# Another order ahead of the first exp in a transformer block kernel: K maxima, transposed tiles, and one copy of K and one of V between ScalarE and VectorE

## The chip, the cores and the metric

The kernel runs on one core of a Trainium2 chip. Its engines work from queues of their own, each strictly in the order of its program, and wait for each other by semaphores: PE (TensorE, matmuls into the eight banks of PSUM), DVE (VectorE), ACT (ScalarE), POOL (GpSimd) and SP (SyncE, which issues the transfers). The metric is the device time of one execution in microseconds, as the median of several runs.

## The reference, cut to what matters

One transformer block in bfloat16 with 2048 tokens of width 640, 32 heads of width 20, and a gated feed-forward part of width 1728.

```python
def _A_ref(x, wqkv, wo):
    qkv = (x @ wqkv).reshape(B, S, 3, H, Dh).transpose(2, 0, 3, 1, 4)
    q, k, v = qkv[0], qkv[1], qkv[2]
    scores = jnp.einsum("bhqd,bhkd->bhqk", q, k) * (Dh ** -0.5)
    p = _softmax(scores, axis=-1)
    o = jnp.einsum("bhqk,bhkd->bhqd", p, v)
    return o.transpose(0, 2, 1, 3).reshape(B, S, D) @ wo

h = x + _A_ref(_layernorm(x), A_wqkv, A_wo)
h2 = h + (gelu(_layernorm(h) @ w_gate) * (_layernorm(h) @ w_up)) @ w_down
```

## The kernel before

**A list scheduler writes the program.** The kernel's Python code describes some 6,900 operations with an engine, an estimated duration, a priority (a smaller number goes first), what they read and write, and the PSUM banks that they take and free. `Sched.schedule` (L100 to L272) plays them through on estimated times and so fixes the order on each engine; `emit` (L274) writes that order with its semaphore waits. On the chip the order is fixed, the times are not: an instruction that waits holds everything behind it on its engine.

**Units and slots.** The scores of 128 keys by 512 queries of one head, or an equal area with fewer queries, are a tile of one PSUM bank. A unit (L1045) takes two or three tiles: PE computes the scores (L1069, four heads at a time in rows of 32 partitions), ACT does one exp over all of them into `pts` or the second ring, which lies in `rege`, and PE multiplies the result with V (PV, recorded at L440). Some tiles go to DVE instead, which forms the exponential out of integer operations (L982 and further rows of L440). Units are grouped into 32 slots by the chunk of queries and the group of four heads: slots 0 to 7 are the first 512 queries, one group of heads each; 8 to 27 are five chunks of 256; 28 to 31 are two of 128. In the profile slot 0 begins at 35.19 us, slot 4 at 134.1, slot 14 at 381.01, and the last exp ends at 842.05. The projections for later heads, the output projection and the feed-forward part of each finished chunk of queries run as background work between the units; the last chunk's stand alone behind the last exp.

**How the scheduler sets the order.** A score matmul has priority 0. When an exp is placed, `due` (L254) is the time from which PE has to stay free for the next scores, `QK_LEAD` ahead of it; background work that would run past `due` is put off. PE has three modes (full, four rows, four columns) with a cost for changing; an operation in another mode is put off until it has waited longer than `PE_AGE` (L177). `SD_AGE` and `SD_ROW` do the same for the scores of DVE's tiles. Each of these is a tuple with an entry per slot.

**Ahead of the first exp.** The normalised input (16 tiles of 128 tokens, `xnp`) is transposed by PE (L665) and copied out of PSUM into `xnT` by ACT (L671) or, for the tiles in `XN_DVE`, by DVE (L674). The first K tile (`proj_k(0)`: the rows of the first heads, all 2048 tokens) is computed in four chunks of 512 tokens, the last cut into 384 and 128 (`KCUT`); each chunk needs the four transposed tiles of its tokens. ACT copies it to SBUF (L785), and DVE takes the maximum of its absolute values (L782): for chunks 0 and 1 from SBUF, for chunks 2 and 3 (`KPS`) from PSUM ahead of ACT's copy, which waits for it. The maximum over the five parts (`kd`, L835) scales a selection matrix (`sel0`, L837); a matmul with it (L881) and a DVE sum (L885, written `('qo', 0, 0)`) give the bound that is subtracted inside the first scores. Only then can the first score matmul run. An exp needs another function table than the copies and square roots before it, so a table load stands in ACT's queue directly in front of the first exp.

The second K tile (`proj_k(1)`, into `osb`) and the second Q tile are computed while this goes on; their copies on DVE wait for the sum of L885 (`HELD`), and chunk 0 of the second K tile was given to ACT (`K1_ACT`, L790). V is projected three token tiles at a time for the first heads (L897); its copies are on DVE (L907), the ones from tile `V_HOLD` on waiting for `HELD` too. SP issues the transfers that spread Q and K over the partitions in the order of its queue: four for Q, one to `q_rows`, sixteen for the first K tile, then the rows of the later tiles.

Of the kernel before, what the change touches and what calls it, by code (L numbers as in the profile page):

```python
# [18 lines left out]
DRAIN = {"pe": 0.165, "act": 0.118, "dve": 0.085, "pool": 0.05, "sp": 0.0}  # L19
WARM_WIN, WARM_MIN = 3.4, 0.5  # L20
PAD_WIN, PAD_MIN = 3.4, 0.42
QK_LEAD = (0.68, 0.72,) + (0.65,) * 4 + (0.72,) * 7 + (0.6,) * 4 + (0.72,) * 6 + (0.68,) * 9
ACT_GAP = .012
PE_AGE = (2.5, 3.0, 5.0, 5.0, 2.5,) + (1.0,) * 4 + (2.0,) + (5.0,) * 3 + (3.0,) * 4 + (5.0, 5.0, 2.0, 2.0,) + (5.0,) * 4 + (1.5, 1.5, 3.5, 3.0,) + (1.5,) * 3
SD_AGE = (0.6, 0.6, 0.3,) + (0.6,) * 6 + (0.8,) + (0.6,) * 5 + (1.0, 0.3, 0.6, 0.8, 0.6, 1.0, 0.5, 1.0, 1.0, 0.5,) + (0.6,) * 7
SD_ROW = (0,) * 5 + (1.0,) + (0.6,) * 3 + (1.5, 0.6, 0.6, 1.5,) + (0.6,) * 16 + (1.0, 0.6, 0,)
STOP = None


# [22 lines left out]
class Sched:  # L52
# [3 lines left out]
    def __init__(self, nc):  # L56
        self.nc = nc
        self.ops = []
        self.lw = {}
        self.rd = {}  # L60
        self.warm = None
        self.pad = None
        self.final = set()
        self.ev = 9
# [35 lines left out]
    def schedule(self):  # L100
# [5 lines left out]
        free_at = [0.0] * 8  # L106
        owner = [None] * 8
# [4 lines left out]
        mode = {e: None for e in ENGINES}  # L112
# [6 lines left out]
        t = 0.0  # L119
# [5 lines left out]
        cur = 0  # L125
        at = lambda v: v[cur] if isinstance(v, tuple) else v
        total = len(ops)
        scores = sum(o.eng == "pe" and o.mode == "row" for o in ops)
        while done < total:
            assert events, "no operation can start"  # L130
# [5 lines left out]
            for e in ENGINES:  # L136
# [8 lines left out]
                while ready[e]:  # L145
                    p, i = heapq.heappop(ready[e])
                    o = ops[i]
                    got = []
                    if e == "pe" and due is not None and o.prio[0] > 0 and t < due < t + o.dur + (MODE_SWITCH[e] if mode[e] not in (None, o.mode) else 0):
                        skipped.append((p, i))  # L150
                        if due not in events:
                            heapq.heappush(events, due)
                        if len(skipped) >= 60:
                            break
                        continue
                    for bk in o.acq:
                        for b in bk.allowed if scores else bk.allowed + bk.after:
                            if owner[b] is None and free_at[b] <= t + 1e-9 and b not in got and b not in kept:
                                got.append(b)
                                break  # L160
                        else:
                            got = None
                            break
                    if got and o.mode == "row" and 0 < p[0] < 1 and scores > 1 and t - o.ready < (
                            at(SD_AGE) if mode[e] != "row" else at(SD_ROW) if row_end[o.rows[0]] > max([row_start + 0.01] + [freed[b] for b in got]) + 0.02 else 0):
                        skipped.append((p, i))
                        continue
                    if got is None:

                        if p[0] == 0:  # L170
                            kept.update(bk.allowed[0] for bk in o.acq)
                        skipped.append((p, i))
                        continue
                    skipped.append((p, i))
                    if chosen is None:
                        chosen, banks = o, got
                        if e != "pe" or p[0] < 1 or p[0] == P_NOW or o.mode == mode[e] or t - o.ready > at(PE_AGE):  # L177
                            break
                    elif o.mode == mode[e]:
                        chosen, banks = o, got  # L180
                        break
                    if len(skipped) >= 60:
                        break
# [34 lines left out]
                scores -= o.eng == "pe" and o.mode == "row"  # L218
                if o.tag and o.tag[0] == "S":
                    cur = self.slot_of[o.tag[1]]  # L220
                if e == "pe" and self.pad is not None and o.tag and o.tag[0] in ("O", "Oq"):
# [146 lines left out]
WN, WB, WW, WC = 76, (5, 4), 256, 32  # L368
KCUT = (384,)
KPS = (2, 3)  # L370
P_VA = 9
VN = 4
D_RING = (9,) * 4 + (6, 6,) + (9,) * 6 + (6,) * 16 + (12,) + (6,) * 3
D_FIRST = 0
# [10 lines left out]
P_V1 = 3.0  # L385
P_V0 = 2.5
P_ON = 2.1
V_ACT = ()
XN_DVE = (8, 10, 13, 15)
VP = (0, 2, 5, 8)  # L390
V1 = ((0, 0, 0, 0, 0, 0, 0, 0, 1, 1, 1, 1, 1, 1, 1, 1), (2, 2, 2, 2, 3, 3, 3, 3, 3, 3, 3, 3, 4, 4, 4, 4))
X_LAT = 3.0
# [4 lines left out]
P_KP = 1.6  # L397
K1_AFTER = 3
Q1_HOLD = 1
V_HOLD = 4  # L400
XD = ()
P_NOW = 1.05
P_K0 = 1.0
VB = (6, 7, 5)
K1_ACT = (0,)
FULL = (5,)
GROUPS = ((0, 4), (4, 7), (11, 5))
AG = (11, 5)
# [10 lines left out]
def bass_sequential_preLN__mha_block__glu_gated_geglu__prompt_kernel(  # L419
# [12 lines left out]
    with ExitStack() as es:  # L432
# [340 lines left out]
        def proj_part(col, t, c, dst, dkey, banks, prio, evac, after, start, lo, hi, k):  # L773
# [6 lines left out]
                                   [("xnT", tt) for tt in range(4 * c + lo // 128, 4 * c + hi // 128)] + ["wqk"], prio, after=start))  # L780
            if dkey[0] == "ku" and t == 0:
                red = lambda src, r: op("dve", lambda eng: eng.tensor_reduce(km[:, c + k:c + k + 1], src(), AX.X, ALU.max, apply_absolute_value=True),  # L782
                                        0.62 if n == 512 else 0.1 + n * 0.00102, P_K0, reads=[r], writes=[("km", c + k)])
                m = [red(lambda: bank(bk, n), key)] if c in KPS else []
                e = op("act", lambda eng: eng.activation(dst, bank(bk, n), ACT.Copy), c_act(n), prio, reads=[key],  # L785
                       writes=[dkey], rel=[bk], after=m)
                if c not in KPS:
                    w_readers.append(red(lambda: dst, dkey))
            elif evac == "act":
                e = op("act", lambda eng: eng.activation(dst, bank(bk, n), ACT.Copy), c_act(n), prio, reads=[key],  # L790
                       writes=[dkey], rel=[bk])
# [253 lines left out]
        def unit(u):  # L1045
# [11 lines left out]
            xd = dtile[u]  # L1057
            six = ring[u]
            al = tl + ([xd] if six else [])
            bks = [Bank(s0 + i) for i in range(len(al))]  # L1060
            fns = []
            reads = []
# [22 lines left out]
            qk = op("pe", fns, 0.215, P_QK, mode="row", util=0.0533 * len(al), rows=tuple(x[3] for x in al), reads=reads, writes=[("S", u), "qkseq"] + ([("SD", xd)] if six else []), acq=bks)  # L1085
            for x in al:
                last_qk[CHUNKS[slots[x[0]][0]][0] // 512].append(qk)
            if six:
# [422 lines left out]
```

## Time and profile before

| | us |
|---|---|
| median of 3 runs (lowest, highest) | 869.43 (868.62, 869.72) |
| the profiled execution, its time | 868.33 |
| its span, first to last instruction | 866.6 |
| ACT busy | 838.3 |
| DVE busy | 748.9 |
| PE busy | 830.7 |

The granted clock of TensorE is 0.998 of full speed on average. A row of the timeline reads: start in us, length in us, engine, line, operation, the tiles written and read with their shapes, the count of equal instructions merged into it, and in brackets how long the engine stood idle before it and what ended that. Instructions of one engine overlap at their ends, so the bars of a merged row add up to more than the time from one start to the next. A row of the busy times by stage reads: the stretch, its length, then busy time and count on PE, on PE's weight loads, on DVE, ACT and POOL, the clock, the share of the DMA engines and GB/s. SPq are the transfers as SP issues them.

### The profile page before, as it was taken

The numbers are of one execution on the slowest core, as the hardware profiler recorded it, in microseconds if no ns is written. First come the engines' busy times: TensorE is split into PE (matmuls) and PEld (weight loads), VectorE is DVE, ScalarE is ACT, GpSimd is POOL, SyncE is SP. The second block draws the span as 40 slices with busy tenths as digits, with TensorE's granted clock in tenths as the row PEclk, the third lists the DMA queues.
The fourth block names the chain that finished last, engine by engine and source line by source line (L and its number), as shares of the span: only waits on it lengthen the run. The fifth ranks groups of instructions, "written<-read, shape, count | busy, mean of one in ns | idle before, by whom it ended". The sixth has DMA issues, their size and how long they took to land.

```text
span 866.6 us, 35475 instructions
## 1 busy us (share of the span) xinstructions
PE 830.7 (96%) x16164; PEld 421.4 (49%) x16199; DVE 748.9 (86%) x1372; ACT 838.3 (97%) x806; POOL 92.2 (11%) x268
## 2 busy tenths in 40 slices
PE   7999999999999899999999999999999999999998
PEld 5533322322344344445455555555554556666667
DVE  8759899999899789697899989999999897998344
ACT  7899999999999999999999999999999999999992
POOL 5001111110001210101102010011102110010000
PEclk9999999999999999999999999999999999999999
DMA  7211122113201752001111201010111201020000
GB/s 273 82 46 59 32 76 61 40 61 93 64 10 46 166 156 83 16 16 30 58 33 28 36 8 61 3 36 16 37 32 19 56 17 28 19 48 11 2 18 17
DMA packets 50173, 43.19 MB, mean 50 GB/s; under 512 B 21316, under 2 KB 44640, under 8 KB 50024
## 3 DMA queue, kind: packets, MB, share of 16 engines
q1 hardware_dynamic: 50024, 40.93, 16.9%
q8 instruction: 127, 2.08, 1.0%
q14 instruction: 22, 0.18, 0.1%
HBM read 27.95 MB, written 10.26 MB: 44 GB/s over the span
## 4 chain that ended last, share of the span: by engine, by line
ACT 57%; PE 35%; DVE 7%; issue 1%
ACT pts L440 38%; ACT rege L440 17%; PE ps L1069 10%; PE ps L743 9%; PE ps L440 8%; PE ps L748 2%; DVE qt_all L440 2%; PE ps L897 1%; PE ps L1324 1%; ACT qt_all L440 1%; PE ps L1393 1%; DVE qt_all L982 1%; DVE rege L440 1%; DVE rege L982 1%; DVE stats L440 1%
## 5 line engine op out<-in xcount | busy, mean ns | idle before, releaser
L440 ACT ACTIVATE pts<-ps 128x1024 bf16<-128x1024 f32 (+1 forms) x496 | 558.7, 1245 | 1.6 <-PE ps L1069 1.0
L1069 PE MATMUL ps<-qt_all,kt_all 32*128 32x256 bf16 (+2 forms) x4096 | 307.2, 272 | 17.8 <-ACT pts L440 9.5
L440 ACT ACTIVATE rege<-ps 128x1024 bf16<-128x1024 f32 (+1 forms) x222 | 248.7, 1205 | 0.4 <-PE ps L1069 0.2
L1069 PEld LDWEIGHTS ps<-qt_all,kt_all 32*128 32x128 bf16 x4096 | 104.2, 92 | 207.4 <-ACT pts L440 94.6
L982 DVE TENSOR_SCALAR rege<-ps 128x512 int16<-128x512 f32 x220 | 148.9, 684 | 17.9 <-PE ps L1069 16.2
L440 PE MATMUL ps<-rege,v_all 128*21 128x256 bf16 (+2 forms) x2197 | 140.1, 286 | 0.1
L440 PE MATMUL ps<-pts,v_all 128*21 128x256 bf16 (+2 forms) x2403 | 124.6, 273 | 0.8 <-DVE osb L440 0.8
L743 PE MATMUL ps<-rege,regw 128*32 128x256 bf16 (+1 forms) x2600 | 119.9, 296 | 1.4 <-DVE rege L982 0.5
L982 DVE TENSOR_SCALAR qt_all<-ps 128x512 int16<-128x512 f32 x128 | 86.7, 683 | 13.4 <-PE ps L1069 12.8
L440 DVE TENSOR_SCALAR rege<-rege 128x2048 int16<-128x2048 int16 x141 | 94.4, 686 | 1.1 <-PE ps L440 0.4
L743 PEld LDWEIGHTS ps<-rege,regw 128*32 128x32 bf16 x2600 | 60.6, 96 | 33.8 <-issue 19.3
L440 PEld LDWEIGHTS ps<-rege,v_all 128*21 128x21 bf16 x2197 | 54.3, 91 | 41.4 <-issue 27.2
L440 PEld LDWEIGHTS ps<-pts,v_all 128*21 128x21 bf16 x2403 | 56.7, 91 | 25.9 <-issue 18.6
L743 PE MATMUL ps<-regw,rege 128*32 128x320 bf16 x1296 | 67.4, 301 | 0.3 <-DVE rege L982 0.3
L440 DVE TENSOR_SCALAR qt_all<-qt_all 128x2048 int16<-128x2048 int16 (+4 forms) x113 | 65.3, 588 | 2.7 <-ACT qt_all L440 1.1
L440 POOL TENSOR_SCALAR rn<-rc 128x16 int32<-128x16 int32 x22 | 8.3, 379 | 461.5 <-DMA rc<-sums 461.4
L440 PE MATMUL ps<-qt_all,v_all 128*21 128x256 bf16 (+1 forms) x1264 | 56.4, 264 | 1.0 <-DVE qt_all L440 0.8
L440 DVE TENSOR_SCALAR qt_all<-rege 128x2048 int16<-128x2048 int16 x80 | 54.0, 686 | 1.8 <-PE ps L440 1.3
L748 PE MATMUL ps<-regw 128*128 128x512 bf16 (+2 forms) x188 | 51.8, 365 | 2.7 <-issue 1.6
L1378 DVE TENSOR_TENSOR rege<-rege,ps 128x512 bf16<-128x512 bf16 (+2 forms) x53 | 35.0, 661 | 13.1 <-PE ps L743 6.7
L1324 PE MATMUL ps<-rege,regw 128*128 128x128 bf16 (+1 forms) x420 | 40.9, 238 | 0.0
L743 PEld LDWEIGHTS ps<-regw,rege 128*32 128x32 bf16 x1296 | 29.9, 96 | 18.3 <-issue 10.6
(139 smaller groups left out, 801.1 us busy)
## 6 DMA issues: line engine op xcount, KB each, us to landing
bsum<-rsums SPq DMA_DIRECT2D x88, 64.0 KB, 2.1
rege<-in_A_x_dram SPq DMA_DIRECT2D x5, 640.0 KB, 5.9
q_rows<-regw SPq DMA_DIRECT2D x20, 128.0 KB, 1.7
out_dram<-rege SPq DMA_DIRECT2D x15, 160.0 KB, 1.8
regw<-in_B_w_gate_dram SPq DMA_DIRECT2D x5, 432.0 KB, 3.9
regw<-in_B_w_up_dram SPq DMA_DIRECT2D x5, 432.0 KB, 3.3
kt_all<-k_rows SPq DMA_DIRECT2D x12, 160.0 KB
qt_all<-q_rows SPq DMA_DIRECT2D x12, 160.0 KB
```

Source lines behind the costliest of these rows:

```text
L440: return lambda eng: getattr(eng, method)(*args, **kwargs)
L743: return [lambda eng, j=j: eng.matmul(out()[32 * j:32 * j + 32], l[:, 32 * j:32 * j + 32], r, start=start, stop=stop, tile_position=(0, 32 ...
L748: fn = col4(lambda: bank(bk, n), l, r, k == 0, k == len(steps) - 1) if col else lambda eng, l=l, r=r, k=k: eng.matmul(bank(bk, n), l, r, s ...
L897: w_readers.append(op("pe", lambda eng, i=i, kt=kt, a=a: eng.matmul(bank(bk)[:, i * w:i * w + w], xnT[:, a, kt * 128:(kt + 1) * 128], wv[: ...
L982: d_ops.append(op("dve", lambda eng: eng.tensor_scalar(v[:, 512 * h:512 * h + 512], bank(b), EXP_MUL, -32000.0, ALU.mult, ALU.max), c_dve( ...
L1069: return lambda eng: eng.matmul(out()[:, kk * nq:(kk + 1) * nq], kt_all[32 * j:32 * j + 32, g, kt * 128:(kt + 1) * 128], qt_all[32 * j:32 ...
L1324: lambda eng, a=a, f=f, fi=fi: eng.matmul(bank(bk)[:, fi * nq:(fi + 1) * nq], w[:, a, F0[f]:F0[f] + 128], hnT[:, a, 128 * tb:128 * tb + nq ...
L1378: hdone.append(op("dve", lambda eng, bu=bu, fv=fv, w=w: eng.tensor_tensor(fv, fv, bank(bu, w), ALU.mult), c_dve(w), p, reads=[ku] + hkeys( ...
L1393: f == NF - 1) if cl else lambda eng, f=f, o=o, bk=bk, w0=w0, w1=w1: eng.matmul(
```

## The change

Ahead of the first exp: the maxima of the first K tile get priority 1.52 (`P_KM`) in place of 1.0, behind the copies of transposed tiles (1.5), except the last one (chunk 3, second part). ACT copies no chunk of the second K tile (`K1_ACT`), so DVE copies all four; ACT copies the V tiles 0 to 2 (`V_ACT`). V copies from tile 3 on wait for `HELD` (before: from 4 on, which with three tiles to a copy let the one of tiles 3 to 5 go). DVE copies the transposed tile 7 in place of 8.

Behind it: new entries per slot in `QK_LEAD`, `PE_AGE`, `SD_AGE` and `SD_ROW`. The scheduler gets a further condition for holding PV work back ahead of scores (with `RESV`, which is 0.0), and the latency of the score matmuls gets a name (`QK_LAT`, 0.165, as before).

```diff
-QK_LEAD = (0.68, 0.72,) + (0.65,) * 4 + (0.72,) * 7 + (0.6,) * 4 + (0.72,) * 6 + (0.68,) * 9
+QK_LEAD = (0.68, 0.72,) + (0.65,) * 4 + (0.72,) * 7 + (0.6,) * 4 + (0.72,) * 6 + (0.68, 0.68, 0.55, 0.55, 0.68, 0.65, 0.65, 0.68, 0.68,)
-PE_AGE = (2.5, 3.0, 5.0, 5.0, 2.5,) + (1.0,) * 4 + (2.0,) + (5.0,) * 3 + (3.0,) * 4 + (5.0, 5.0, 2.0, 2.0,) + (5.0,) * 4 + (1.5, 1.5, 3.5, 3.0,) + (1.5,) * 3
-SD_AGE = (0.6, 0.6, 0.3,) + (0.6,) * 6 + (0.8,) + (0.6,) * 5 + (1.0, 0.3, 0.6, 0.8, 0.6, 1.0, 0.5, 1.0, 1.0, 0.5,) + (0.6,) * 7
-SD_ROW = (0,) * 5 + (1.0,) + (0.6,) * 3 + (1.5, 0.6, 0.6, 1.5,) + (0.6,) * 16 + (1.0, 0.6, 0,)
+PE_AGE = (2.5,) + (3.0,) * 5 + (5.0,) * 8 + (3.0,) * 3 + (5.0, 5.0, 2.0, 2.0,) + (5.0,) * 4 + (1.5, 1.5, 3.5, 3.0,) + (1.5,) * 3
+SD_AGE = (0.6, 0.6, 0.3,) + (0.6,) * 6 + (0.8,) + (0.6,) * 5 + (1.0, 0.3, 0.6, 0.8, 0.6, 1.0, 0.5, 1.0, 1.0, 0.5,) + (0.6,) * 3 + (0.8,) * 4
+SD_ROW = (0,) * 5 + (0.6,) * 4 + (1.5, 0.6, 0.6, 1.5,) + (0.6,) * 16 + (1.0, 0.6, 0,)
...
+                    if (got and e == "pe" and at(RESV) and p[0] >= 1 and nextu in self.with_d and due is not None and due - t < at(RESV)
+                            and not any(owner[b] is None and free_at[b] <= t + 1e-9 and b not in got for b in self.d_banks)):
+                        skipped.append((p, i))
+                        continue
...
+P_KM = 1.52
+RESV = 0.0
+QK_LAT = 0.165
...
-V_ACT = ()
-XN_DVE = (8, 10, 13, 15)
+V_ACT = (0,)
+XN_DVE = (7, 10, 13, 15)
...
-V_HOLD = 4
+V_HOLD = 3
...
-K1_ACT = (0,)
+K1_ACT = ()
...
-                                        0.62 if n == 512 else 0.1 + n * 0.00102, P_K0, reads=[r], writes=[("km", c + k)])
+                                        0.62 if n == 512 else 0.1 + n * 0.00102, P_K0 if c + k == 3 + len(KCUT) else P_KM, reads=[r], writes=[("km", c + k)])
...
-            qk = op("pe", fns, 0.215, P_QK, mode="row", ..., acq=bks)
+            qk = op("pe", fns, 0.215, P_QK, mode="row", ..., acq=bks, lat=QK_LAT)
```

More of the change, by code (lines that the diff above doesn't have):

```diff
@@ L61, in __init__ @@
         self.warm = None
+        self.with_d, self.d_banks = set(), (5, 7)
         self.pad = None
@@ L127, in schedule @@
         total = len(ops)
+        nextu = 0
         scores = sum(o.eng == "pe" and o.mode == "row" for o in ops)
@@ L220, in schedule @@
                     cur = self.slot_of[o.tag[1]]
+                    nextu = o.tag[1] + 1
                 if e == "pe" and self.pad is not None and o.tag and o.tag[0] in ("O", "Oq"):
@@ L1059, in unit @@
             al = tl + ([xd] if six else [])
+            if xd and not six:
+                sc.with_d.add(u)
             bks = [Bank(s0 + i) for i in range(len(al))]
@@ L1084, in unit @@
                         reads += qk_reads(x)
-            qk = op("pe", fns, 0.215, P_QK, mode="row", util=0.0533 * len(al), rows=tuple(x[3] for x in al), reads=reads, writes=[("S", u), "qkseq"] + ([("SD", xd)] if six else []), acq=bks)
+            qk = op("pe", fns, 0.215, P_QK, mode="row", util=0.0533 * len(al), rows=tuple(x[3] for x in al), reads=reads, writes=[("S", u), "qkseq"] + ([("SD", xd)] if six else []), acq=bks, lat=QK_LAT)
             for x in al:
```

## The prediction

> **What bounds the kernel now.** I read first the page's span, busy line and chain, then busy time by stage, cut at the first exp, at the start of slot 14 and at the end of the last exp.
>
> ```profile
> span 866.6 us, 35475 instructions
> PE 830.7 (96%) x16164; PEld 421.4 (49%) x16199; DVE 748.9 (86%) x1372; ACT 838.3 (97%) x806; POOL 92.2 (11%) x268
> ACT 57%; PE 35%; DVE 7%; issue 1%
> ...
> 0.00:35.19 35.19, 28.91 (x250) 21.27 (x253) 29.69 (x86) 25.55 (x47) 11.70 (x31) 0.95 0.51 182
> 35.19:381.01 345.82, 327.06 (x4410) 122.94 (x4441) 304.32 (x519) 344.71 (x318) 35.34 (x105) 1.00 0.24 67
> 381.01:842.05 461.04, 453.06 (x11215) 259.06 (x11214) 403.09 (x736) 460.11 (x428) 45.21 (x132) 1.00 0.11 29
> 842.05:866.60 24.55, 21.67 (x299) 18.15 (x296) 11.77 (x32) 7.93 (x15) 0.00 (x0) 0.99 0.05 15
> ```
>
> The fourth figure of a stage is ACT. From the first exp at 35.19 to the last at 842.05 ACT stands idle for 1.11 and 0.93 us: the softmax exps follow each other, and 97% is an average over a saturated middle and two loose ends. So this kernel can be shortened by an earlier first exp, by less work on ACT behind it, or in the last 24.55 us. The ACT timeline shows what precedes the first exp:
>
> ```profile
> 23.63 1.31 ACT L671 ACTIVATE regw<-ps 128x640 bf16<-128x640 bf16 x2
> 24.79 0.63 ACT L785 ACTIVATE regw<-ps 128x512 bf16<-128x512 f32 x1
> 25.95 1.30 ACT L671 ACTIVATE regw<-ps 128x640 bf16<-128x640 bf16 x2 [0.53 <-PE ps L665]
> 27.14 0.60 ACT L785 ACTIVATE regw<-ps 128x512 bf16<-128x512 f32 x1
> 27.71 0.70 ACT L671 ACTIVATE regw<-ps 128x640 bf16<-128x640 bf16 x1
> 29.53 1.07 ACT L785 ACTIVATE regw<-ps 128x512 bf16<-128x512 f32 x2 [1.11 <-DVE km L782]
> 31.41 0.28 ACT L785 ACTIVATE regw<-ps 128x128 bf16<-128x128 f32 x1 [0.81 <-DVE km L782]
> 33.28 0.60 ACT L790 ACTIVATE osb<-ps 128x512 bf16<-128x512 f32 x1 [1.59 <-PE ps L748]
> 33.90 1.28 ACT L440 ACT_TABLE_LOAD   x1
> 35.19 5.97 ACT L440 ACTIVATE pts<-ps 128x1536 bf16<-128x1536 f32 x5
> ...
> 32.00 0.38 PE L881 MATMUL ps<-regw,sel 128*128 128x512 bf16 x1
> 33.32 0.60 PE L1069 MATMUL ps<-qt_all,kt_all 32*128 32x512 bf16 x5
> ```
>
> The scores of the first unit start at 33.32, and with 0.38 us for a matmul of 512 columns and some 0.05 to the reader its exp could have begun at about 33.76. It begins at 35.19, because the table load stands in ACT's queue behind the second K tile's copy (33.28), which waits for PE. So 1.43 us are lost to the order on ACT, and the rest hangs on the scores at 33.32.
>
> **The change part by part: what does nothing.** The new hold in the scheduler asks for RESV above zero, which is 0.0; QK_LAT is PE's old drain value, 0.165. In the instruction orders of the two kernels PE, DVE, ACT and SP run the same sequence from slot 14 on, except four rows moved on PE and two on DVE in slot 29, so the late entries of QK_LEAD, SD_AGE and PE_AGE cost nothing. ACT's order differs only before the first exp. The effect is therefore the shift of the first exp, plus what slots 0 to 13 do with it.
>
> **ACT before the first exp.** The second K tile's copy is gone from ACT, and the copy of V tiles 0 to 2 stands behind the K copy of 24.79. A 512-column copy there took 0.60, the next starting some 0.57 later. The V copy (480 columns) fills 25.37 to 25.94, nearly all in the 0.53 us in which ACT waited for transposes.
>
> **The chain of the K maximum.** DVE's rows before:
>
> ```profile
> 23.51 0.49 DVE L674 COPY regw<-ps 128x640 bf16<-128x640 bf16 x1 [0.38 <-PE ps L665]
> 24.01 0.25 DVE L440 TENSOR_SCALAR regw<-regw 128x512 int16<-128x512 int16 x1
> 24.48 0.49 DVE L674 COPY regw<-ps 128x640 bf16<-128x640 bf16 x1 [0.22 <-PE ps L665]
> 24.89 1.15 DVE L440 TENSOR_SCALAR rege<-rege,mu,rs 128x640 bf16<-128x640 bf16 x3
> 25.95 0.68 DVE L782 TENSOR_REDUCE km<-regw 128x1 f32<-128x512 bf16 x1
> 27.66 0.65 DVE L907 CAST v_all<-ps 128x480 bf16<-128x480 f32 x1
> 28.82 1.26 DVE L782 TENSOR_REDUCE km<-ps 128x1 f32<-128x512 f32 x2
> 30.00 0.48 DVE L674 COPY regw<-ps 128x640 bf16<-128x640 bf16 x1
> 31.09 0.29 DVE L782 TENSOR_REDUCE km<-ps 128x1 f32<-128x128 f32 x1
> 31.41 0.16 DVE L440 TENSOR_REDUCE kd<-km 128x1 f32<-128x5 f32 x1
> 31.61 0.51 DVE L440 TENSOR_SCALAR sel<-sel,kd 128x4 bf16<-128x4 bf16 x2
> 32.49 0.75 DVE L885 SCALAR_TENSOR_TENSOR qt_all<-ps,off,qt_all 128x512 bf16<-128x512 f32 x1 [0.38 <-PE ps L881]
> ...
> 22.55 0.44 PE L665 MATMUL ps<-ident,rege 128*128 128x128 bf16 x5
> 28.51 0.98 PE L748 MATMUL ps<-regw 128*128 128x384 bf16 x5
> 29.53 1.52 PE L748 MATMUL ps<-regw 128*128 128x512 bf16 x9
> 30.89 1.06 PE L897 MATMUL ps<-regw 128*128 128x160 bf16 x13
> ```
>
> Bars of one engine overlap, so I step by start to start: a transposed copy 0.40, a normalised tile 0.35, a maximum of 512 columns 0.6 to 0.7, one of 384 about 0.56; on PE five transposes take 0.28, five 512-column matmuls 1.08. Before, the copy of tile 15 (30.00) stands behind a V copy and three maxima; its matmuls and the last maximum (31.09) follow. Walked in the new order: copy of tile 7 at 23.03 (its transposes end at 22.99); tile 10 normalised 23.44; reciprocal and absolute value to 24.2; tiles 11 and 12 to 24.9; copy of tile 10 at 24.99 (0.5 later than before, PE's transposes now stand behind two K matmuls); tiles 13, 14, 15 at 25.40, 25.75, 26.11; copy of tile 13 at 26.62; first maximum 27.02; copy of tile 15 at 27.61, 2.4 earlier.
>
> On PE the third K chunk's matmuls wait for ACT's copy of tile 11 (now 25.94 to 26.65) and end at 28.30; the fourth's 384 columns wait for ACT's copy of tile 14 (to 27.78), start at 28.14, and with the last 128 columns end at 29.39. DVE's remaining maxima run 28.34, 28.93, 29.53, 29.74 and end at 30.30: kd at 30.33 against 31.41, 1.08 earlier. From kd the old rows repeat: sel0 to 30.76; the bound's matmul at 30.86, when PE leaves the Q matmuls queued ahead of it; the DVE sum 31.35 to 32.10; scores at 32.17 (fifteen V matmuls of 0.069 on PE end at 32.11); exp at 32.61. On ACT the last two K copies wait for the maximum that ends at 30.30, and run to 31.13; the load takes 31.15 to 32.43 and is hidden by 0.2. First exp: **32.61 against 35.19, 2.58 us earlier**, of which 1.43 is the table load and 1.15 the chain.
>
> Bounds: the load alone, with the chain no earlier, gives 1.43; the chain's first possible exp is held by the load, and with DVE's 0.3 us pause before 28.34 gone it gives about 2.85. I take 2.58, the walk being made of this kernel's own rows.
>
> The load row is where a rule speaks against. The Trainium skill, "ScalarE: Activation LUTs", section "What ACT_TABLE_LOAD costs", puts a switch of sets at about 1283 ns and a drain of 1380 more, 2.66 us in all. By this the first exp would stand at 33.81, and the gain would be 1.38. This trace has the first exp 1.29 after the load's start.
>
> **Moved behind the first exp.** The V copies from tile 3 on now wait for the DVE sum. Behind them on DVE stand the Q copy, the next V copy and the K copies; the second K tile's first five matmuls wait for the bank that the V copy frees, so 1.08 us of PE work and a DVE copy, about as long as the V copy's 0.65, move into slot 0.
>
> ```profile
> 25.45 11.98 SPq L440 DMA_DIRECT2D kt_all<-regw  x16
> 37.48 0.95 SPq L440 DMA_DIRECT2D k_rows<-osb  x2
> ```
>
> That tile's first transfer leaves SP only at 37.48, behind sixteen K transfers, which covers the later copy. PE and DVE have the slack: from 35.19 to 381.01 PE is idle for 18.8 us, DVE for 41.5. Without the cover it would be one late unit of scores, at most the 1.08 us themselves. I take 0, the transfer's row being the nearest.
>
> **Slots 0 to 13 rearranged.** PE's ages rise from 1 or 2 us to 3 to 5 in slots 5 to 9. Such a plan can misfire on the chip, as here:
>
> ```profile
> 137.48 1.03 PE L748 MATMUL ps<-regw 128*128 128x512 bf16 x4 [0.19 <-issue]
> 138.98 0.60 PE L1069 MATMUL ps<-qt_all,kt_all 32*128 32x512 bf16 x6
> 139.41 3.71 ACT L440 ACTIVATE pts<-ps 128x1536 bf16<-128x1536 f32 x3 [0.95 <-PE ps L1069]
> ```
>
> Background matmuls held PE, the scores came late, and ACT lost 0.95 of the 1.11 us it loses before slot 14. The new order may drop this event (up to 1.1 gained) or make another (1.1 lost); I take 0. In the orders the transfer of slot 4's query bounds stood five exps ahead of its first use and now stands four ahead; at 344.71 us for 318 ACT instructions that is 1.1 us less margin and 4.3 left.
>
> **Sum.** The profiled execution took 868.33, with 1.73 us around its span; the runs' median is 869.43, 1.10 above it, so I keep the difference. 868.33 - 2.58 = 865.75; against the median **866.9 us**.
>
> **Rivals.** (a) The plan's event at 139.41 does not come back: 2.58 + 1.1 = 3.7 earlier, 865.7. For it: slot 4's order on PE is new. Against: one slot of 31 shows such an event, others may.
> (b) The chain ends no earlier, only the load is uncovered: 868.0. For it: four maxima now stand together at the end, and a third K chunk 1.1 us late undoes their start. Against: the V copy fits ACT's idle time.
> (c) The load takes ACT for its length a second time before the exp: 31.15 + 2 x 1.28 = 33.71, 867.95. For it speaks no row; against it, 33.90 + 1.28 = 35.18 and the exp at 35.19. The skill's page named above states such a drain.
> (d) Slower: PE, held in order by background matmuls that waited up to 5 us and then for banks which DVE frees late, misses scores in slots 5 to 9. The price is 1.1 for each event; from the third on the gain is eaten, and with four the time is 869.43 - 2.58 + 4.5 = 871.4. For it: the event above; against: the ages of 5.0 already stand in slots 10 to 12, in a stretch with 0.16 us of other ACT idle.
> (e) The start moves and is given back before slot 14, by two events or by late bounds in slot 4: 869.4.
>
> **How the numbers follow.** Forecast 0.52 (866.2 to 867.7), (a) 0.14, (b) 0.16, (c) 0.03, (d) 0.08, (e) 0.07. What a measurement can tell from no change is 0.2%, 1.74 us here, so "faster" ends at 867.7: 0.50 of the forecast, (a), and 0.02 of (b) give 0.66; (d) and a little of (e) 0.09 slower; 0.25 the same. The range 864.6 to 869.4 goes from (a) with a further event gone to half of (e).
>
> **What would show it.** Right: no L790-like copy ahead of the load, the load at about 31.2, first exp near 32.6, kd near 30.3, slot 14's first exp near 378.4, and the same 485 us from there to the end. Wrong: scores later than the load's end by over half a microsecond (the chain is mis-sized), a gap behind the load (c), or ACT idle for over 2 us between the first exp and slot 14 (d, e).

## The result, and the profile after

The changed kernel takes 867.26 us as the median of 15 runs (866.01 to 868.03), the kernel before 868.83 in the 15 runs beside it (868.0 to 869.77). The ratio is 0.9981, with a 95% interval from 0.9974 to 0.9989: 1.57 us faster, between 0.95 and 2.3. The forecast of 2.58 less had the direction; about a microsecond of it did not arrive. The profiled execution took 867.75 us.

The page's span, busy line and chain, and the busy times of the same four stages as before, cut at the first exp, at slot 14 and at the last exp:

```profile
span 866.0 us, 35545 instructions
PE 838.5 (97%) x16215; PEld 420.4 (49%) x16215; DVE 750.4 (87%) x1372; ACT 838.4 (97%) x806; POOL 89.6 (10%) x268
ACT 51%; PE 39%; DVE 8%; issue 1%
...
0.00:32.84 32.84, 27.00 (x242) 20.37 (x242) 27.65 (x82) 25.25 (x47) 11.71 (x31) 0.95 0.53 193
32.84:379.18 346.34, 335.56 (x4465) 122.69 (x4468) 307.57 (x524) 344.96 (x319) 33.52 (x105) 1.00 0.24 67
379.18:841.49 462.31, 454.26 (x11218) 259.23 (x11212) 403.40 (x736) 460.29 (x429) 44.34 (x132) 1.00 0.11 28
841.49:866.00 24.51, 21.67 (x299) 18.14 (x295) 11.78 (x32) 7.94 (x15) 0.00 (x0) 1.00 0.04 15
```

The first exp moved from 35.19 to 32.84, 2.35 earlier. But from there to slot 14 it now takes 346.34 us (345.82 before), and from slot 14 to the last exp 462.31 (461.04). Of 2.35 us, 0.5 went back in the first part and 1.27 in the second, where both kernels run the same orders but for a few rows. ACT's and DVE's timelines ahead of the first exp, to be read against those of the prediction:

```profile
25.01 0.63 ACT L795 ACTIVATE regw<-ps 128x512 bf16<-128x512 f32 x1
25.49 0.62 ACT L915 ACTIVATE v_all<-ps 128x480 bf16<-128x480 f32 x1
25.94 1.95 ACT L681 ACTIVATE regw<-ps 128x640 bf16<-128x640 bf16 x3
...
30.51 0.80 ACT L795 ACTIVATE regw<-ps 128x384 bf16<-128x384 f32 x2 [0.66 <-DVE km L792]
31.33 1.28 ACT L450 ACT_TABLE_LOAD   x1
32.84 1.45 ACT L450 ACTIVATE pts<-ps 128x1536 bf16<-128x1536 f32 x1 [0.23 <-PE ps L1081]
...
27.83 0.48 DVE L684 COPY regw<-ps 128x640 bf16<-128x640 bf16 x1
...
30.51 0.16 DVE L450 TENSOR_REDUCE kd<-km 128x1 f32<-128x5 f32 x1
```

The V copy (25.49) fills what had been a wait. The table load follows ACT's last K copy and is over at 32.61; the exp then waits 0.23 for the scores. Tile 15's copy stands at 27.83 and kd at 30.51; the prediction's walk through the rows had 27.61 and 30.33. The whole start of this execution lies some 0.2 later than that of the old profile (a pair of transposed copies on ACT that both kernels have begins at 23.84 in place of 23.63), so the walk held to about 0.05.

Where ACT then waits for scores, in the changed kernel's ACT timeline:

```profile
160.51 5.54 ACT L450 ACTIVATE pts<-ps 128x1536 bf16<-128x1536 f32 x5 [0.67 <-PE ps L1081]
...
197.29 2.37 ACT L450 ACTIVATE rege<-ps 128x1536 bf16<-128x1536 f32 x2 [0.17 <-PE ps L1081]
...
220.25 1.02 ACT L450 ACTIVATE pts<-ps 128x1024 bf16<-128x1024 f32 x1 [0.20 <-PE ps L1081]
...
744.48 2.00 ACT L450 ACTIVATE pts<-ps 128x1024 bf16<-128x1024 f32 x2 [0.42 <-PE ps L1081]
749.03 5.97 ACT L450 ACTIVATE pts<-ps 128x1536 bf16<-128x1536 f32 x5 [0.30 <-PE ps L1081]
...
765.14 5.65 ACT L450 ACTIVATE pts<-ps 128x1536 bf16<-128x1536 f32 x5 [0.42 <-PE ps L1081]
```

The old event at 139.41 is gone; a new one stands in slot 5, with small ones in slots 6 and 7, two in slot 28 and one in slot 29 (765.14). The experiments ask what these places are.

### The profile page after: what moved, and what is told of

Read it like the earlier page. It is cut to its first block, busy times and chain, and to the rows that moved or that the text cites. A ratio compares the mean times of both kernels' runs of the same rounds, so it can differ in the third digit from the quotient of the medians.

```text
span 866.0 us, 35545 instructions
## 1 busy us (share of the span) xinstructions
PE 838.5 (97%) x16215; PEld 420.4 (49%) x16215; DVE 750.4 (87%) x1372; ACT 838.4 (97%) x806; POOL 89.6 (10%) x268
## 3 DMA queue, kind: packets, MB, share of 16 engines
q8 instruction: 127, 2.08, 1.0%
## 4 chain that ended last, share of the span: by engine, by line
ACT 51%; PE 39%; DVE 8%; issue 1%
ACT pts L450 35%; ACT rege L450 15%; PE ps L1081 11%; PE ps L450 10%; PE ps L753 9%; PE ps L758 3%; DVE qt_all L450 2%; DVE rege L450 2%; PE ps L907 1%; PE ps L1336 1%; DVE rege L992 1%; DVE qt_all L992 1%; PE ps L1405 1%; ACT qt_all L450 1%; PE ps L675 1%
## 5 line engine op out<-in xcount | busy, mean ns | idle before, releaser
L1081 PE MATMUL ps<-qt_all,kt_all 32*128 32x256 bf16 (+2 forms) x4096 | 304.0, 273 | 11.5 <-ACT pts L450 5.6
L758 PE MATMUL ps<-regw 128*128 128x512 bf16 (+2 forms) x215 | 59.6, 368 | 0.4
```

The source lines that it names most:

```text
L758: fn = col4(lambda: bank(bk, n), l, r, k == 0, k == len(steps) - 1) if col else lambda eng, l=l, r=r, k=k: eng.matmul(bank(bk, n), l, r, s ...
L1081: return lambda eng: eng.matmul(out()[:, kk * nq:(kk + 1) * nq], kt_all[32 * j:32 * j + 32, g, kt * 128:(kt + 1) * 128], qt_all[32 * j:32 ...
```

## The experiments

The table has, for every profile, the first exp's time and the lengths from the first exp of a stretch of slots to the first exp behind it, read off ACT's timeline. The kernels were not all timed on one chip, so what compares is the ratio to the kernel before, which ran beside each.

| kernel | first exp | slots 0-10 | slot 11 | slots 28+29 | time, us | ratio (95%) |
|---|---|---|---|---|---|---|
| before | 35.19 | 265.34 | 23.96 | 47.77 | 868.83 | |
| before_again | 34.94 | 265.32 | 24.54 | 48.03 | 868.98, one run | |
| after | 32.84 | 265.94 | 23.92 | 49.02 | 867.26 | 0.9981 (0.9974-0.9989) |
| again | 32.44 | 265.95 | 23.91 | 49.60 | 867.41 | 0.9977 (0.9967-0.9986) |
| after_c | 31.94 | 265.92 | 23.92 | 48.71 | 867.75 | 0.9979 (0.9970-0.9988) |
| late_old | 32.51 | 265.97 | 23.91 | 49.21 | 867.74 | 0.9981 (0.9972-0.9990) |
| pro_only | 32.34 | 266.20 | 27.94 | 48.44 | 868.83 | 0.9998 (0.9989-1.0006) |
| tab_only | 34.50 | 265.33 | 24.88 | 49.18 | 869.98 | 1.0005 (0.9996-1.0014) |
| k1_only | 33.87 | 265.32 | 24.75 | 48.94 | 868.23 | 0.9982 (0.9972-0.9991) |
| shift32 | 32.49 | 265.93 | 25.73 | 48.22 | 866.92 | 0.9969 (0.9958-0.9979) |
| shift64 | 31.94 | 265.95 | 23.91 | 47.99 | 866.43 | 0.9967 (0.9955-0.9979) |
| shift64_b | 32.92 | 265.99 | 23.93 | 48.59 | 866.83 | 0.9968 (0.9957-0.9980) |
| aft_nokm | 32.66 | 265.93 | 23.93 | 49.76 | 868.36, one run | |
| aft_noV | 33.94 | 265.22 | 24.19 | 48.69 | 868.19, one run | |

Slots 12 to 27 differ by at most 0.2 us in all fourteen. So all that these kernels differ in lies in four places: the first exp, slots 0 to 10, slot 11, and slots 28 and 29.

**The changed kernel again (again).** No edit.

> The changed kernel once more, nothing edited. In its first profile the last exp stood 486.83 us, with the tail, before the end of the span, against 485.59 in the kernel before: 1.0 us of it in slot 28 (24.65 us against 23.64) and 0.25 in slot 29, though up to slot 29 both kernels run the same orders there. Theory A (that loss belongs to one execution): this profile has slot 28 near 23.6 and 485.6 +- 0.3 from slot 14's first exp to the end; the time differs from 867.26 by less than 0.5. Theory B (it belongs to the changed kernel): slot 28 is again near 24.6, and 486.8 us again. Both: first exp at 32.6 to 32.9, slot 14's first exp at 378.7 to 379.3.

Theory B held: slot 28 took 25.18 us, and the loss is there again, so it is no accident of one execution. The rows of PE's weight loads show where it arises:

```profile
742.48 0.12 PEld L753 LDWEIGHTS ps<-regw,rege 128*32 128x32 bf16 x8
742.63 0.10 PEld L753 LDWEIGHTS ps<-wda,rege 128*32 128x32 bf16 x3
743.63 0.09 PEld L753 LDWEIGHTS ps<-wda,rege 128*32 128x32 bf16 x1 [0.90 <-issue]
743.87 0.23 PEld L1081 LDWEIGHTS ps<-qt_all,kt_all 32*128 32x128 bf16 x12
...
744.32 2.00 ACT L450 ACTIVATE pts<-ps 128x1024 bf16<-128x1024 f32 x2 [0.69 <-PE ps L1081]
```

Between the third and the fourth of four like weight loads 0.90 us passed without a load and with no semaphore to wait for ("issue"), and ACT waited 0.69 for the scores behind them. In the first profile it is the same place, with 0.62. What PE can lack there is its own program. The transfers in the microsecond from 741.2 on, of the same kernel:

```profile
q8 instruction: 1, 0.02, 5.8%
```

One packet of 16 KB on the queue of instructions, 5.8% of sixteen engines' time, that is 0.93 us; the trace has it from 741.22 to 742.16, and the fourth load begins at 743.63, 1.48 us after its end. The page counts 127 such packets with 2.08 MB; with 16215 weight loads, as many matmuls and some 140 waits on PE, that is a block of 16 KB for 256 instructions. This became theory F: in slots 28 and 29 PE waits for its instructions.

**The late entries taken back (late_old).**

```diff
-QK_LEAD = ... (0.72,) * 6 + (0.68, 0.68, 0.55, 0.55, 0.68, 0.65, 0.65, 0.68, 0.68,)
+QK_LEAD = ... (0.72,) * 6 + (0.68,) * 9
-SD_AGE = ... + (0.6,) * 3 + (0.8,) * 4
+SD_AGE = ... + (0.6,) * 7
```

> The changed kernel with the kernel before's QK_LEAD and SD_AGE, which differ from slot 25 on and move four rows on PE and two on DVE in slot 29; nothing else is altered. Theory B (the late entries cost the missing microsecond): slots 28 and 29 take 23.6 and 24.1 us, and the time is 1.0 to 1.2 below that of the changed kernel, near 866.1. Theory A (one execution): the time is within 0.4 of the changed kernel's, and slots 28 and 29 show a loss in neither or in both by chance.

The time is within 0.4 of the changed kernel's, slot 28 takes 25.19: the moved rows of slot 29 are not the cause.

**Only the start, and only the tables (pro_only, tab_only).**

pro_only is the changed kernel with the four tables QK_LEAD, PE_AGE, SD_AGE and SD_ROW of the kernel before; tab_only is the kernel before with these four tables of the changed kernel.

> Only the part ahead of the first exp: the changed kernel with QK_LEAD, PE_AGE, SD_AGE and SD_ROW of the kernel before. Theory (the ages of slots 0 to 13 are worth nothing on balance): first exp at 32.6 to 32.9, slot 4 loses its 1.44 us over the pace again, slot 5 is back at 0.43, first exp to slot 14 takes 345.8 +- 0.3, and the time is within 0.4 of the changed kernel's. Rival 1 (the changed ages cost the half microsecond that the first profile showed more in slots 0 to 13, 346.33 against 345.82, and the late entries another): the time is 865.9 to 866.4, the prologue's whole 2.35 to 2.58 below the kernel before. Rival 2 (the new start needs the new ages): an event of 1 us or more in slots 0 to 9 that neither kernel has, 868 or above.

> The other half: the kernel before with QK_LEAD, PE_AGE, SD_AGE and SD_ROW of the changed kernel, the start as before. First exp at 35.2 to 35.4. Theory (the tables are worth nothing on balance): 868.8 +- 0.4. Rival 1 (they cost 0.5 in slots 0 to 13 and about 1 in slots 28 and 29): 869.9 to 870.4. Rival 2 (they are a gain with the old start, the event in slot 4 gone): 867.7 to 868.0.

The halves do not add up. With the old tables the same early start is worth nothing (0.9998), and with the old start the new tables are worth nothing either (1.0005). The theory for pro_only failed in its details: slots 4 and 5 are as in the changed kernel (23.94 and 24.58), so what changed there comes with the start and not with the ages. tab_only says the same: with the new ages and the old start slots 4 and 5 are as before (24.74 and 23.72). And pro_only's loss is where none of the expectations had it, in slot 11. Rows of pro_only: PE; SP, with what SP waited for from 270 to 310 us (us in all, times, longest); busy times by stage (behind POOL's stands the granted clock):

```profile
305.33 0.40 PE L753 MATMUL ps<-rege,regw 128*32 128x512 bf16 x4 [1.74 <-DMA regw<-in_B_w_gate_dram]
...
298.54 3.72 SPq L450 DMA_DIRECT2D regw<-in_B_w_gate_dram  x2
SPq L450 <- DMA regw<-in_B_w_gate_dram: 10.5, 5, 3.0
...
304.00:306.00 2.00, 0.67 (x12) 0.23 (x13) 0.00 (x0) 0.85 (x1) 0.00 (x0) 0.98 0.53 186
306.00:308.00 2.00, 2.00 (x23) 0.62 (x20) 1.44 (x3) 1.02 (x1) 0.00 (x0) 0.50 0.75 222
```

The same place in before_again and in k1_only, and SP's row of again:

```profile
305.15 0.40 PE L743 MATMUL ps<-rege,regw 128*32 128x512 bf16 x4 [0.39 <-DMA regw<-in_B_w_gate_dram]
...
304.30 0.40 PE L743 MATMUL ps<-rege,regw 128*32 128x512 bf16 x4 [0.61 <-DMA regw<-in_B_w_gate_dram]
...
299.20 0.35 SPq L450 DMA_DIRECT2D regw<-in_B_w_gate_dram  x1
```

Gate weights come in pieces that follow one another; SP waits five times for one of them to land before it goes on. In pro_only the last one that PE needs is issued at 301.91, though its slot 11 begins 2.0 us earlier than in the first profile of before (298.54 and 300.53), where it is issued at 301.49. The chain of transfers hardly moved with the exps, and PE, which gets there sooner, waits longer: 0 in before, 0.39 in before_again, 0.38 in tab_only, 0.61 in k1_only and 1.74 in pro_only, where slot 11 begins 0.3, 0.7, 1.3 and 2.0 us earlier than in before. In the changed kernel the tables, on top of the new start, give an order in which the last of these issues is at 299.20 (again), and PE has no such wait. This profile of pro_only is the slowest of its runs (870.97; the median is 2.1 lower), and not all of its loss in slot 11 is the gate weights': ACT waits 0.45 us ahead of them (301.57), 1.24 with them (306.10) and 1.79 behind (308.91). From 305.94 on PE ran for 3.41 us at half clock, to which the last wait is put down here; that was not tried, and a second profile was not taken. The Trainium skill, "TensorE: Matmul & The Clock Gate", Part 1, has freely running windows of 3413 ns and a halved clock after an idle one; this trace agrees in the length and with 0.50, but the window before, 302.53 to 305.94, was not idle: PE was busy for 1.55 of its 3.41 us.

**The kernel before again, and its second K copy alone (before_again, k1_only).** k1_only differs from the kernel before in one line:

```diff
-K1_ACT = (0,)
+K1_ACT = ()
```

> The kernel before once more, for its spread. Slots 0 to 10 and 14 to 27 within 0.1 us of its first profile. Theory F and a late weight transfer in slot 11 (as the kernel with only the new tables showed, 0.92 us there): slot 11 at 23.95 or up to 1 us longer, slots 28 and 29 at 23.6 to 25.3 us each, the total between 868.2 and 870.5. Rival (the kernel before always keeps 23.64 and 24.12 in slots 28 and 29, and the loss belongs to the changed kernels): both slots within 0.1 us of that.

> The kernel before with one edit, K1_ACT empty: the second K tile's copy leaves ACT, so the table load no longer stands behind it; maxima, V copy and tables as before. The load should start when ACT's last K copy ends (31.7), be over at 33.0, and the first exp follow the scores: 33.76 plus up to 0.2 of start offset, 1.43 earlier than 35.19. Rival of a load that takes its length twice: 31.7 + 2 x 1.28 = 34.3. The time: 868.83 - 1.43 = 867.4 against a kernel before at 868.83 if all of it reaches the end; within 0.4 of the kernel before if, as with the changed kernel's start under the old tables, slot 11 and slots 28 and 29 eat it.

The kernel before keeps its slots 0 to 10 to 0.02 us; slot 11 and slots 28 and 29 vary (24.54, 24.01 and 24.02), so its own figures there are not fixed either. ACT's rows of k1_only:

```profile
31.53 0.28 ACT L785 ACTIVATE regw<-ps 128x128 bf16<-128x128 f32 x1 [0.81 <-DVE km L782]
31.82 1.28 ACT L440 ACT_TABLE_LOAD   x1
33.87 2.37 ACT L440 ACTIVATE pts<-ps 128x1536 bf16<-128x1536 f32 x2 [0.77 <-PE ps L1069]
```

The first exp stands at 33.87, with kd 0.12 later than in the old profile: 33.75 against the 33.76 of the sum, so the uncovered load was 1.43 us. ACT is free at 33.10 and waits for the scores, which a load of double length would not have shown. Of this gain 1.37 us reached the median; the profiled execution (868.98, the slowest of the ten runs) lost 0.8 in slot 11 and 1.2 in slots 28 and 29 against before.

**The ranking and the V copy, each taken away (aft_nokm, aft_noV).**

```diff
 aft_nokm
-P_KM = 1.52
+P_KM = 1.0
 aft_noV
-V_ACT = (0,)
-V_HOLD = 3
+V_ACT = ()
+V_HOLD = 4
```

> The changed kernel with P_KM = 1.0: the maxima rank with the last again, so that DVE takes the first before tile 13's copy and the second before tile 15's; no K copy ahead of the load and the V copy on ACT, as in the changed kernel. Theory (DVE's summed work decides; what was taken off it, the V copies, brought kd forward, and the ranking alone little): kd and the first exp within 0.3 us of the changed kernel's (30.3 and 32.6 without start offset). Rival (the ranking brings the 1.15 us, since the third K chunk's matmuls stand behind the copy of tile 15, which moves back 0.7): kd near 31.0, the first exp near 33.3.

> The changed kernel without the V copy on ACT (V_ACT empty, V_HOLD 4): DVE makes that copy between the last maximum and kd, the ranking as in the changed kernel. Theory (what left DVE brought kd forward): one V copy's 0.6 us back on the chain, kd near 30.9, the first exp near 33.2, both without start offset. Rival (the ranking does it all): kd at 30.3 and the first exp at 32.6.

DVE's and ACT's rows of aft_nokm, then of aft_noV:

```profile
28.41 0.49 DVE L684 COPY regw<-ps 128x640 bf16<-128x640 bf16 x1
28.82 1.45 DVE L792 TENSOR_REDUCE km<-ps 128x1 f32<-128x512 f32 x3
30.30 0.16 DVE L450 TENSOR_REDUCE kd<-km 128x1 f32<-128x5 f32 x1
...
32.66 3.71 ACT L450 ACTIVATE pts<-ps 128x1536 bf16<-128x1536 f32 x3 [0.40 <-PE ps L1081]
```

```profile
30.52 0.65 DVE L917 CAST v_all<-ps 128x480 bf16<-128x480 f32 x1
31.09 0.15 DVE L450 TENSOR_REDUCE kd<-km 128x1 f32<-128x5 f32 x1
31.15 0.65 DVE L917 CAST v_all<-ps 128x480 bf16<-128x480 f32 x1
31.71 0.50 DVE L450 TENSOR_SCALAR sel<-sel,kd 128x4 bf16<-128x4 bf16 x2
...
33.94 1.45 ACT L450 ACTIVATE pts<-ps 128x1536 bf16<-128x1536 f32 x1 [1.20 <-PE ps L1081]
```

Without the ranking the copy of tile 15 moves back (28.41), but kd stands at 30.30, earlier than in the changed kernel by 0.21, nearly all of it start offset, that is, a whole start that lies earlier or later (0.18 by the copy of tile 10): ranked or not, DVE has the same work ahead of kd and hardly a pause. So with the V copies gone from DVE, the ranking of the maxima is worth nothing. Without the edit on V, two V copies stand around kd (30.52 and 31.15), and the first exp, freed of a start that lies 0.49 later (by the copy of tile 10, 25.48 against 24.99 in the walk), comes at 33.45: 0.82 of the 1.15 us is the V copies. That is more than the 0.6 expected, since the second copy also stands ahead of the selection matrix. k1_only's 33.75 is 0.30 above it, the worth of the rest (the ranking and tile 7 for tile 8) while V is on DVE.

The same profile settles slots 0 to 10: with V back on DVE they take 265.22 us again, although the new tables stand. The 0.6 us that the changed kernel loses there come with the edit on V. Slot by slot against before, the new event costs 0.85 in slot 5 and the missing old one saves 0.79 in slot 4, so these two nearly cancel. The 0.60 is what many small delays leave: +0.29, +0.43, +0.15 and +0.25 in slots 3, 6, 7 and 8, -0.15, -0.24 and -0.24 in slots 0, 1 and 9. Little of it shows as idle time: ACT's idle time in slots 0 to 10 grew by about 0.2 us, the rest is exps that begin 0.1 to 0.3 us later behind the one before them, with which they overlap less. What delays each of these was not followed up. The largest place, slot 5, in rows of again, DVE and then ACT:

```profile
157.22 0.67 DVE L875 TENSOR_SCALAR regw<-ps 32x512 bf16<-32x512 f32 x1
157.82 2.10 DVE L992 TENSOR_SCALAR rege<-ps 128x512 int16<-128x512 f32 x3
...
160.10 5.54 ACT L450 ACTIVATE pts<-ps 128x1536 bf16<-128x1536 f32 x5 [0.67 <-PE ps L1081]
```

A bound of the queries goes in ahead of three tiles of exponentials on DVE; PE's next scores wait for their bank, and ACT for the scores. That it is the bound's 0.67 us which makes them late is read from the order, and not shown.

**PE's instruction blocks moved (shift32, shift64, shift64_b, after_c).** More instructions ahead of 13 us, where PE waits, move the borders of all later blocks against the work:

```diff
-            wb = Bank(*WB)
-            op("pe", lambda eng, wb=wb: eng.matmul(PS[:, 512 * wb.b:512 * wb.b + WW], ...
+            wb, ws = Bank(*WB), (128, 128) if i < 32 else (WW,)
+            op("pe", [lambda eng, wb=wb, w=w: eng.matmul(PS[:, 512 * wb.b:512 * wb.b + w], ...
```

This is shift32; in shift64 and shift64_b the tuple is (86, 85, 85), and after_c is the changed kernel without an edit.

> The changed kernel, with each of the first 32 warm-up matmuls of 256 columns cut into two of 128: 32 weight loads and 32 matmuls more on PE before 13 us, in time in which PE waits anyway; every order behind is the changed kernel's. Theory F (in slots 28 and 29 PE waits for its own instructions, which arrive 16 KB at a time, 128 weight loads and 128 matmuls to a block): every place where PE stops without a wait of its own lies 32 weight loads earlier in the work, so that the stop after the third of the four matmuls of L753 on wda in slot 28 (weight load 13474 of the program) is gone and stops, where there are any, come at weight loads 13474, 13601, 13857 and so on of the new count, 1.3 to 1.6 us after a block has landed; the loss of slots 28 and 29 together (1.2 to 1.5 us in three profiles) becomes another one, anywhere from 0 to 3. Rival (something in slot 28's own work stops PE): the stop is at the same four matmuls, 0.6 to 0.9 us long, and the time within 0.3 of the changed kernel's.

> As the run before it, with the first 32 warm-up matmuls cut into three, so that 64 weight loads and 64 matmuls are added. Theory F: block borders lie 64 weight loads earlier in the work than in the changed kernel; stops in slots 28 and 29, where there are any, come at the same numbers of the new count, and the loss of the two slots is between 0 and 3 us; the rest of the kernel differs by less than 0.3 us. Rival: the stop at the four matmuls of L753 on wda, again 0.6 to 0.9 us, and the time within 0.3 of the changed kernel's.

> The changed kernel a third time, unedited, as the measure for the next one. Theory F: stops in slots 28 and 29 at weight loads 13474 and 13601 as in its two profiles before, these slots together 49.0 to 49.7 us; 2.0 us below the kernel before, as the second time. Rival (luck of single executions): 48 us together.

> The changed kernel with 64 weight loads and matmuls more in the warm-up, a second time, on the same chip as the unedited one. Theory F: slots 28 and 29 together at 48.0 +- 0.3 again, no stop there, and a time 0.9 to 1.4 us below the unedited kernel's. Rival (the first time was luck): within 0.4 us of the unedited kernel, slots 28 and 29 near 49 us.

In shift32 the four matmuls run through without a stop, and the only stop of PE in slots 28 and 29 lies elsewhere (PE's weight loads, then PE):

```profile
744.51 0.11 PEld L753 LDWEIGHTS ps<-wda,rege 128*32 128x32 bf16 x4
...
779.21 0.34 PE L450 MATMUL ps<-pts,v_all 128*21 128x128 bf16 x10 [0.26 <-issue]
```

All places from slot 28 on where more than 0.4 us passed on PE ahead of a weight load that has no wait of its own, by that load's number in the program (for the shifted kernels in the new count), and the time from the end of the instruction transfer before it, both read off the records of the trace:

| kernel | weight load | less 13474, in blocks of 127.67 | us after the block landed |
|---|---|---|---|
| aft_nokm | 13347, 13601 | -0.99, 0.99 | 1.40, 1.45 |
| after | 13474, 13601 | 0, 0.99 | 1.41, 1.33 |
| again | 13474, 13601 | 0, 0.99 | 1.48, 1.50 |
| late_old | 13474, 13601 | 0, 0.99 | 1.31, 1.51 |
| after_c | 13474, 13857 | 0, 3.00 | 1.42, 1.44 |
| k1_only | 13473, 14112 | -0.01, 5.00 | 1.36, 1.47 |
| shift64_b | 13729, 14240 | 2.00, 6.00 | 1.39, 1.44 |
| tab_only | 13856, 14112 | 2.99, 5.00 | 1.52, 1.38 |
| aft_noV | 14111 | 4.99 | 1.49 |
| pro_only | 14367 | 6.99 | 1.51 |
| shift32 | 14623 | 9.00 | 1.51 |

Eleven profiles have their stops on one grid, that of whole blocks (the step that fits is 127.67 loads: with as many matmuls and a few waits, 256 instructions), always 1.3 to 1.5 us after a block has landed; the three left (before, before_again, shift64) have none, and the two slots are shortest in them. A smaller stop fits as well: the changed kernel's wait of 0.42 at 765.14 follows a stop of 0.40 at weight load 14112, 5.00 blocks on, 1.53 us after a block. That is theory F, and the rival of a cause in slot 28's work falls with shift32. Two details were wrong: after_c has its second stop at another border, with 48.71 us for the slots in place of at least 49.0, and shift64_b has two stops where none was expected (48.59). A place on the grid makes a stop possible, and small differences of time decide whether it comes. The borders without a stop fit too: with all borders of slots 28 and 29 placed by that step (in aft_nokm one load later), PE passes none of the 169 in the fourteen profiles sooner than 1.26 us after the last block has landed.

The times: the shifted kernels stand at 0.9967 to 0.9969 of the kernel before, the unshifted at 0.9977 to 0.9981, 0.92 us apart on the chip that ran both (866.83 and 867.75). Any two of these intervals overlap; that all three comparisons lie on one side is what speaks for it. shift64 has the lowest ratio of all, by less than the noise.

## Why the prediction was right, and where a microsecond went

The forecast time, 866.9, is within 0.4 us of the 867.26 measured, but that it is so close is luck: the kernel before took 868.83 beside it, 0.6 less than the 869.43 from which the sum starts, and the gain came out 1.0 smaller, so the two misses nearly cancel. The terms one by one:

- **What bounds the kernel** (ACT from the first exp on): right. Every idle stretch of ACT over 0.1 us between the first exp and slot 14 is a wait for scores, and so are the losses in slots 28 and 29.
- **The first exp, 2.58 earlier**: right. It is 2.35 in the profiled pair. Executions whose start runs at full clock have 31.94 and 34.50 (changed start, old start), 2.56 apart.
- **The load, 1.43**: right, k1_only has it alone. Rival (c) and the rule of the Trainium skill ("ScalarE: Activation LUTs", "What ACT_TABLE_LOAD costs", a drain of 1380 ns behind the load) fall: in the changed kernel the exp begins 1.51 us after the load's start, 0.23 of that a wait for PE.
- **The chain, 1.15**: right in size; its parts were read otherwise. The V copies carry 0.82 and the ranking nothing once they are gone. The walk added up DVE's rows correctly without asking which of the edits had made the room.
- **Moved behind the first exp, 0**: right for the place that it looked at. Slot 0 takes 27.86 us, 28.00 before. The edit on V does cost something, but later, in the next point.
- **Slots 0 to 13, 0 within 1.1**: within its bounds, but for another reason than the one given. Rival (a)'s event did go, another came in slot 5, and with small delays around them slots 0 to 10 cost +0.60 in all three profiles. The prediction put such a rearrangement down to PE's new ages; it comes with the edit on V (aft_noV has none of it with the new ages, pro_only has it with the old ones). In slot 11 the changed kernel gains up to 0.6, for before_again lost that to its gate weights.
- **From slot 14 on "the same 485 us", as the orders are the same**: this is the step that failed. From slot 14's first exp to the end the profile takes 486.8 us, 485.6 before. Equal orders fix what PE does, not when its instructions arrive. The changed kernel issues 16 weight loads more (16215 against 16199; 4710 against 4694 up to slot 14 in the rows by stage), and block borders lie that much earlier in the same work. Slots 28 and 29 take 48.7 to 49.6 us in its three profiles, 47.8 and 48.0 in the two of before, a loss of 0.7 to 1.8.

Of the rivals, (b) and (c) fall by the two points on the start; (e) and (d) asked for two and four events of 1.1 us before slot 14, and there is one, of 0.67.

Summed over the profiles (first exp at like clock, slots 0 to 10, slot 11, slots 28 and 29, each by its means), -2.5 + 0.6 - 0.3 + 1.2 is -1.0; the timed runs say -1.57, -2.02 and -1.95. The two profiles of the kernel before may be lucky ones in slots 28 and 29: kernels with its 16199 loads (k1_only, tab_only, aft_noV) show 48.9, 49.2 and 48.7. How much of the loss there the extra 16 loads cause, and how much is chance, stays open.

## What to carry to other kernels

A start brought forward is worth its time only if everything that the engines meet later comes forward too: a chain of transfers that wait for each other need not move with the compute, and the wait that it hid comes out (slot 11 under the old tables). Where an engine issues many short instructions, the same order does not mean the same time; look for idle "issue" in the middle of a group, and compare with the packets on the instruction queue. And take the edits of a change apart before giving each its share: here the ranking of the maxima was worth nothing beside the others, and the loss behind the start came from the V copy and not from the tables.

## What the runs showed of the hardware

- **Instructions can run short.** In slots 28 and 29 the transfer of a block of 256 instructions takes 0.9 to 1.8 us over the fourteen profiles, and PE has gone past a border no sooner than some 1.3 us after a block had landed (1.26 at the least). In again the block that PE lacked began its transfer at 741.22, 1.6 us after PE had passed the border before (739.62), and PE went on at 743.63: 4.0 us for one block. In slots 14 to 27 a block lasts about 5.3 us in that profile (the median from border to border, the borders placed by the step above), in slots 28 and 29, with half as many columns to a score matmul, about 3.9. Busy times of again in slot 27 and in slot 28 (the weight loads are the second count):

```profile
702.00:706.00 4.00, 3.87 (x102) 2.13 (x102) 3.97 (x9) 4.00 (x5) 0.00 (x0) 1.00 0.07 14
740.00:744.00 4.00, 3.44 (x132) 2.38 (x129) 2.76 (x6) 3.63 (x4) 0.00 (x0) 1.00 0.01 4
```

That is 102 loads in 4 us, and 129, a whole block, in spite of the stop. The Trainium skill, "Runtime: NRT & Kernel Launch", section "Instruction fetch mechanics", has the 16 KiB blocks, which agrees with 2.08 MB in 127 packets, and calls the cost of crossing a border mostly hidden; here it shows with stops of up to 1.0 us.
- **The clock at the start differs from one execution to the next.** The changed kernel's stretch up to the first exp has a granted clock of 0.95 in its first profile (the row 0.00:32.84 above) and of 1.00 in after_c, and the first exp stands at 32.84 and 31.94. again has 0.95 as well and 32.44, so of such a difference of 0.5 to 0.9 us some 0.4 can have another cause. The clock records of the traces show what goes with it. In eleven of the fourteen profiles the first stretch at full clock begins at 5.57 to 7.93 us, lasts 6.83 and is followed by 3.41 us at half clock; in the three others (after_c, tab_only, shift64) it begins at 8.06 to 8.55, and no half clock follows. In the 3.41 us ahead of each half-clock stretch up to the last exp, pro_only's included, PE was busy for 0.3 to 1.65 us; between the first full clock and the last exp, no window of that length on the same grid in which it was busy for 1.78 us or more was followed by one (the 1.65 is aft_noV's, the 1.78 shift64's). In the first fifteen runs of the changed kernel the five at a full clock took 866.01 to 867.26, the ten others 866.61 to 868.03. Of after_c's eleven runs the two fastest (866.16 and 866.56) are the two at a full clock; of again's nine, the fastest (866.85) and the sixth (867.73).

```profile
0.00:31.94 31.94, 26.56 (x239) 19.60 (x242) 27.37 (x82) 25.19 (x48) 11.71 (x31) 1.00 0.55 198
```
- **A slot can wait for another transfer each time.** In shift32 slot 11 lost 1.8 us though no gate weights were late: DVE waited for the reciprocal sums, where again waits 0.38. Rows of shift32 and of again:

```profile
304.64 0.69 DVE L450 TENSOR_TENSOR on<-osb,bsum 128x512 bf16<-128x512 f32 x1 [2.25 <-DMA bsum<-rsums]
...
302.75 0.69 DVE L450 TENSOR_TENSOR on<-osb,bsum 128x512 bf16<-128x512 f32 x1 [0.38 <-DMA bsum<-rsums]
```
